# A rounded query copied behind the last scores instead of behind the matmuls, and relu's two instructions issued ahead of the chunk's output

## The chip, the cores and the metric

The kernel runs on one core of a Trainium2 chip. The metric is the device time of one execution in microseconds (us), lower is better; the time of a kernel is the median of several executions. Engines are named as in the profile: PE (matmul), PEld (its weight loads), DVE, ACT and POOL (elementwise work), SP (which issues the DMAs). Each engine works through its own queue in order.

## What is computed

Eight batches of eight heads of causal attention with a decay, over 576 tokens of 64 channels, and behind it a layer norm with a two-layer network of width 512 to 2048 and back, with a residual:

```python
scores = (q @ k.T) / 8 + cum[:, None] - cum[None, :]     # cum = cumsum(log(clip(f)))
attn = softmax(where(causal, -1e9, scores))
x = (attn @ v) laid out as (batch, 576, 512)
out = x + max(layernorm(x) * g @ w_ch1, 0) @ w_ch2
```

## The kernel before, in words

**Two kinds of work on one PE.** The kernel interleaves the attention of 64 heads with the network, which takes 18 chunks of 256 tokens (`NCHUNK`), each in 16 steps of 128 hidden channels (`FT`). Time is cut into slots: a head has four, t = 1 to 4, and slot t computes the scores of the row block t (slot 1 those of blocks 1 and 0; block 4 is 128 rows by 576 columns). Beside its attention each slot carries one step of the network, so that a chunk ends every 16 slots, which is every fourth head. After the last head the remaining steps run by themselves.

**What sets the order.** Nothing reorders the instructions: `ORDERS` (line 51) holds strings of letters, and the loop over the slots calls `piece(c)` for every letter of the string that holds at that slot. Letters issue instructions on several engines; on each engine they stand in the order of the string. The third string holds from slot 67 on, the fourth slot of head 16. Heads 0 to 15 (`NFULL`) do their matmuls in full float32. From head 16 on, the operands are split into a rounded part and a remainder; these heads are called late heads here.

**The letters that matter**, for a late head n in slot t:
- `Q`: `qk_mm`. Two matmuls for each block: `hi` against `hi` (L384, rounded q over the remainder of q, against rounded k twice) and `kl` against `xq` (L385, the remainder of k and two rows of the decay, against rounded q and two rows of ones). `xq` is one buffer for all heads.
- `S`, `e`, `B`: softmax. DVE adds the mask and takes the maximum (L425, twice for block 4, whose columns come in two halves), ACT the exponential (L436), DVE the reciprocal of the sum (L441, L442), POOL the product (L443).
- `T`, `d`, `V`: DVE transposes the last slot's block (L463, L465), SP writes it to HBM (L478) and reads it back transposed two slots on (L486).
- `H`, `l`, `o`: the transposed block is rounded by ACT (L501); its remainder comes from DVE (L506) and POOL (L515, two instructions).
- `F`, `a`: ACT copies half of a finished attention output (L649), DVE adds the other half (L660).
- `M`: the 12 matmuls of the first layer's step (L699 to L701), each taking 128 channels of `x`, rounded or remainder.
- `N`: `moe.second()`, the 6 matmuls of the second layer (L721 to L723) of the step before; at the chunk's end also `chunk_out`: two DVE instructions on `acc` (L798) and their DMAs.
- `A`: attention times values (L608), in slots 1 and 3.
- `P`: rounds the values on DVE (L362), in slot 2.
- `x`: `queries_copy`, in slot 4: ACT copies rounded q of the next head from `hi` to `xq` (L353), 64 x 576.
- `r`, `m`: relu of the first layer, rounded by ACT (L707), and its remainder by DVE (L712). Both read the PSUM tile of `M`; the next slot's `N` reads what they write.
- `b`: statistics of the rows; `R`: `moe.rest()`, with the split of the next chunk's `x` (L682 on ACT, L684 on DVE); at the chunk's end it splits the last two tiles, which the next slot's `M` needs.
- `k`: in slots 1 and 3 the next head's k or q is rounded (L339, L347 on ACT) and its remainder taken (L342, L356 on POOL), from a DMA into the single buffer `raw` (L325).

Of the kernel before, what the change touches and what calls it, by code (L numbers as in the profile page):

```python
# [50 lines left out]
ORDERS = [  # L51
    (0, "WwQsSthAeMrgFBmlLNPaXRf"),
    (37, "WwkQSTstAMhPeHlgNFrxfmBoDLRbaXdV"),
    (67, "kQSTeBHloFaMNAPxrmbRLdDVX"),
]


# [1022 lines left out]
```

## Time and profile before

| what | us |
|---|---|
| median of 3 runs (lowest to highest) | 1253.78 (1245.69 to 1289.03) |
| the profiled execution's own time | 1248.68 |
| its span, first to last instruction | 1246.9 |
| PE busy in the span | 1150.8 |
| DVE, ACT, POOL busy | 759.5, 641.0, 633.9 |
| late heads' slots, about | 214 to 1017 us of the span |

Rows of the timeline read: start, duration, engine, line, operation, output and inputs, shape; in brackets how long the engine was idle just before, and what released it. Matmuls overlap, so the end of one is modelled and lies behind the start of the next.

### The profile page before, as it was taken

Reading aid. Unit: us, or ns where it says so; the run is one execution under the profiler, and the core shown is the slowest. Engines: PE = TensorE matmul, PEld = TensorE weight load, DVE = VectorE, ACT = ScalarE, POOL = GpSimd, SP = SyncE. Lnnn points to the kernel's source line nnn. Section 1 sums busy time; section 2 is a strip of 40 time slices with the busy share of each in tenths; the row PEclk is TensorE's granted clock in tenths of the full one; section 3 lists DMA queues with packets and bytes.
Section 4 is the critical chain, followed back from the end, with each engine's and each line's share of the span. In section 5 each row is a group of like instructions: output and inputs, shape, how many; then the busy total and the mean of one; then the engine's idle time right before and its main releaser. Section 6 shows DMA issues by size and latency. Waiting matters only on the chain.

```text
span 1246.9 us, 24808 instructions
## 1 busy us (share of the span) xinstructions
PE 1150.8 (92%) x7648; PEld 1017.4 (82%) x7648; DVE 759.5 (61%) x2706; ACT 641.0 (51%) x1648; POOL 633.9 (51%) x966
## 2 busy tenths in 40 slices
PE   8889999999888999989899989898998999999998
PEld 6557888888787888888788878787887889999997
DVE  6777773666767766767667676766776762222222
ACT  5887575545555555655555555555555542112111
POOL 3545344566657666666666666666666551000000
PEclk9999999999999999999999999999999999999999
DMA  6555532657676776767675767677776751110100
GB/s 187 148 153 168 141 109 64 182 164 204 181 198 190 208 194 188 206 178 216 184 212 168 219 177 211 171 217 194 201 190 197 215 155 50 52 34 18 51 27 26
DMA packets 252724, 194.80 MB, mean 156 GB/s; under 512 B 83888, under 2 KB 231344, under 8 KB 252592
## 3 DMA queue, kind: packets, MB, share of 16 engines
q1 hardware_dynamic: 252592, 193.22, 55.7%
q8 instruction: 61, 1.00, 0.3%
q14 instruction: 71, 0.58, 0.2%
HBM read 126.79 MB, written 66.36 MB: 155 GB/s over the span
## 4 chain that ended last, share of the span: by engine, by line
PE 57%; ACT 14%; DVE 11%; DMA 7%; issue 7%; POOL 2%; SPq 1%; ACTq 0%; DVEq 0%; POOLq 0%
PE h L699 7%; PE h L700 7%; PE h L701 7%; PE acc L721 7%; PE acc L722 7%; PE acc L723 7%; PE o L608 5%; ACT ph L501 5%; ACT p L436 3%; DVE p L425 3%; PE s L385 2%; DMA pd<-pb 2%; ACT xq L353 2%; ACT ot L649 2%; PE s L384 2%
## 5 line engine op out<-in xcount | busy, mean ns | idle before, releaser
L436 ACT ACTIVATE p<-p,st 64x64 f32<-64x64 f32 (+4 forms) x320 | 179.2, 560 | 343.6 <-DVE st L425 284.9
L443 POOL TENSOR_SCALAR p<-p,st 64x64 f32<-64x64 f32 (+4 forms) x320 | 171.1, 539 | 360.6 <-DVE st L442 231.7
L700 PE MATMUL h<-x,w1h 128*128 128x256 f32 x1152 | 327.9, 285 | 5.0 <-DVE x L684 5.0
L699 PE MATMUL h<-x,w1h 128*128 128x256 f32 x1152 | 331.2, 287 | 0.6 <-DVE st L425 0.4
L701 PE MATMUL h<-x,w1l 128*128 128x256 f32 x1152 | 325.9, 283 | 0.0
L712 DVE SCALAR_TENSOR_TENSOR hh<-h,hh 128x256 fp32r<-128x256 f32 x288 | 121.4, 421 | 208.8 <-ACT hh L707 208.7
L721 PE MATMUL acc<-w2h,hh 128*128 128x512 f32 x576 | 230.6, 400 | 0.1
L722 PE MATMUL acc<-w2l,hh 128*128 128x512 f32 x576 | 229.8, 399 | 0.0
L700 PEld LDWEIGHTS h<-x,w1h 128*128 128x128 f32 x1152 | 219.9, 191 | 10.6 <-DVE x L684 7.5
L723 PE MATMUL acc<-w2h,hh 128*128 128x512 f32 x576 | 226.9, 394 | 0.0
L699 PEld LDWEIGHTS h<-x,w1h 128*128 128x128 f32 x1152 | 219.3, 190 | 6.6 <-issue 0.9
L701 PEld LDWEIGHTS h<-x,w1l 128*128 128x128 f32 x1152 | 220.4, 191 | 0.0
L707 ACT ACTIVATE hh<-h 128x256 fp32r<-128x256 f32 x288 | 109.0, 378 | 181.4 <-PE h L701 178.4
L425 DVE CUSTOM_DVE_ANT_0 p<-s,mask 64x64 f32<-64x64 f32 (+4 forms) x320 | 130.5, 422 | 100.7 <-PE s L385 93.6
L515 POOL TENSOR_TENSOR pt<-pt,ph 128x128 fp32r<-128x128 f32 x192 | 186.1, 987 | 6.9 <-ACT ph L501 6.9
L385 PE MATMUL s<-kl,xq 66*128 66x288 f32 (+4 forms) x288 | 82.8, 309 | 55.3 <-ACT xq L353 55.3
L723 PEld LDWEIGHTS acc<-w2h,hh 128*128 128x128 f32 x576 | 109.7, 190 | 25.5 <-DVE hh L712 0.2
L721 PEld LDWEIGHTS acc<-w2h,hh 128*128 128x128 f32 x576 | 110.6, 192 | 14.6 <-ACT hh L707 0.3
L722 PEld LDWEIGHTS acc<-w2l,hh 128*128 128x128 f32 x576 | 110.7, 192 | 12.1
L385 PEld LDWEIGHTS s<-kl,xq 66*128 66x128 f32 (+1 forms) x288 | 52.3, 181 | 71.1 <-ACT xq L353 68.7
L784 POOL TENSOR_SCALAR sv<-sv 128x2 f32<-128x2 f32 x18 | 3.9, 214 | 199.5 <-DVE sv L768 199.4
L501 ACT CAST ph<-pt 128x768 fp32r<-128x768 f32 x96 | 94.0, 979 | 5.0 <-DMA pt<-pd 4.5
(86 smaller groups left out, 1891.0 us busy)
## 6 DMA issues: line engine op xcount, KB each, us to landing
raw<-in_qk_dram SPq DMA_DIRECT2D x96, 288.0 KB
pt<-pd SPq DMA_DIRECT2D x192, 144.0 KB
pd<-pb SPq DMA_DIRECT2D x96, 192.0 KB
pt<-pd SPq DMA_DIRECT2D x192, 96.0 KB
wr<-in_w_dram SPq DMA_DIRECT2D x32, 512.0 KB
pd<-pb SPq DMA_DIRECT2D x48, 320.0 KB
pd<-pb SPq DMA_DIRECT2D x48, 256.0 KB
vr<-in_v_dram SPq DMA_DIRECT2D x64, 160.0 KB
```

Of the source, the lines that this page charges most:

```text
L385: mm(sp, xq, kl, start=False, stop=True)
L425: nc.vector.tensor_tensor_reduce(out=pt[:m, a:z], in0=sp, in1=mask[:m, max(0, off + a) : max(0, off + a) + z - a], scale=-SCALE, scalar=3. ...
L436: nc.scalar.activation(pt[:m, :w], pt[:m, :w], AF.Exp, bias=st[:m, i : i + 1], scale=-1.0, accum_out=st[:m, 2:3])
L443: nc.gpsimd.tensor_scalar(out=pt[:m, :w], in0=pt[:m, :w], scalar1=st[:m, 3:4], scalar2=1.0, op0=ALU.mult, op1=ALU.mult)
L501: nc.scalar.copy(out=h.ph[t], in_=h.pt[t].bitcast(F32))
L515: nc.gpsimd.tensor_tensor(out=pt[:, :, r, :], in0=pt[:, :, r, :].bitcast(F32), in1=ph[:, :, r, :].bitcast(F32), op=ALU.subtract)
L699: mm(ph, w1h[:, k, fs], c.x[k][:, 0, :], start=(k == 0), stop=False)
L700: mm(ph, w1h[:, k, fs], c.x[k][:, 1, :], start=False, stop=False)
L701: mm(ph, w1l[:, k, fs], c.x[k][:, 0, :], start=False, stop=(k == KT - 1))
L721: mm(c.acc[i], h[:, 0, ts_], w2h[:, j, :], start=(j == 0), stop=False)
L722: mm(c.acc[i], h[:, 0, ts_], w2l[:, j, :], start=False, stop=False)
L723: mm(c.acc[i], h[:, 1, ts_], w2h[:, j, :], start=False, stop=(j == FT - 1))
```

## The change

One string of `ORDERS` is changed, the one that holds from slot 67 to the end:

```diff
@@ -51,7 +51,7 @@
 ORDERS = [
     (0, "WwQsSthAeMrgFBmlLNPaXRf"),
     (37, "WwkQSTstAMhPeHlgNFrxfmBoDLRbaXdV"),
-    (67, "kQSTeBHloFaMNAPxrmbRLdDVX"),
+    (67, "kQxSTeBHloFaMPrmNAbRLdDVX"),
 ]
```

`x` moves from behind `P` to right behind `Q`. `P`, `r` and `m` move ahead of `N` and `A`. The rows of PE, POOL and SP stand in the same order as before; only ACT and DVE have rows that moved.

On ACT, the fourth slot of a late head, which is also the last step of a chunk; before (`p_4` is the block of scores, `ph` the rounded transposed block, `ot` the half output, `hh` the relu's output, `x_2` and `x_3` the next chunk's last tiles):

```order
L707 ACTIVATE hh_14_10016<-h_14_9991 128x256
L436 ACTIVATE p_4_10036,st_4_10037<-p_4_10036,st_4_10037 128x576
L501 CAST ph_45_10046<-pt_45_9971 128x1152
L649 COPY ot_0_10051<-o_2_10010 64x320
L353 CAST xq<-hi_9846 64x576
L707 ACTIVATE hh_15_10074<-h_15_10054 128x256
L682 CAST x_2_10077<-xr_2_9717 128x256
L682 CAST x_3_10080<-xr_3_9777 128x256
```

and the same place with the change:

```order
L707 ACTIVATE hh_14_10004<-h_14_9991 128x256
L353 CAST xq<-hi_9846 64x576
L436 ACTIVATE p_4_10037,st_4_10038<-p_4_10037,st_4_10038 128x576
L501 CAST ph_45_10047<-pt_45_9971 128x1152
L649 COPY ot_0_10052<-o_2_10013 64x320
L707 ACTIVATE hh_15_10068<-h_15_10055 128x256
L682 CAST x_2_10077<-xr_2_9717 128x256
L682 CAST x_3_10080<-xr_3_9777 128x256
```

The copy to `xq` (L353) has moved up three rows, ahead of the exponential; the relu and the splits stand one row nearer to the exponential. This happens in the fourth slot of 47 heads.

On DVE, the first slot of the next head, where the finished chunk is put out; before (`xt` is the chunk's output, `acc` its PSUM sums):

```order
L441 TENSOR_SCALAR st_0_9173<-st_0_9173 64x1
L442 RECIPROCAL st_0_9173<-st_0_9173 64x1
L798 SCALAR_TENSOR_TENSOR xt_0_8898<-acc_0_8324,rs_8901,xt_0_8898 128x512
L798 SCALAR_TENSOR_TENSOR xt_1_9024<-acc_1_8325,rs_8901,xt_1_9024 128x512
L712 SCALAR_TENSOR_TENSOR hh_0_9218<-h_0_9185,hh_0_9218 128x256
L425 ISA p_2_9227,st_2_9228<-s_2_0_9224,mask 128x320
```

and with the change:

```order
L441 TENSOR_SCALAR st_0_9173<-st_0_9173 64x1
L442 RECIPROCAL st_0_9173<-st_0_9173 64x1
L712 SCALAR_TENSOR_TENSOR hh_0_9198<-h_0_9185,hh_0_9198 128x256
L798 SCALAR_TENSOR_TENSOR xt_0_8898<-acc_0_8329,rs_8901,xt_0_8898 128x512
L798 SCALAR_TENSOR_TENSOR xt_1_9024<-acc_1_8330,rs_8901,xt_1_9024 128x512
L425 ISA p_2_9227,st_2_9228<-s_2_0_9224,mask 128x320
```

The relu's remainder (L712) has changed places with the two output instructions (L798). It does so at 12 chunk ends; `P`'s rounding of the values meets no other DVE row and stays where it stood.

## The prediction

> **What bounds the kernel now.** I read the page's first part, then the list of who waited for whom, then the timeline of one head engine by engine.
>
> ```profile
> span 1246.9 us, 24808 instructions
> PE 1150.8 (92%) x7648; PEld 1017.4 (82%) x7648; DVE 759.5 (61%) x2706; ACT 641.0 (51%) x1648; POOL 633.9 (51%) x966
> ```
>
> PE is busy for all but 1246.9 - 1150.8 = 96.1 us, and no other engine is above 61%. So a change pays only as far as it shortens PE's idle time. The list of waits says where that lies in the late heads:
>
> ```profile
> PE s L385 <- ACT xq L353: 55.3, 46, 2.1
> PE o L608 <- POOL vv L365: 15.2, 12, 1.3
> PE h L700 <- DVE x L684: 5.0, 12, 0.4
> ```
>
> (Total us, times, longest.) The largest wait is for the copy that the change moves. It comes 46 times, so in all but two of the late heads. The next two come 12 times each, once for each chunk's end. The timeline of an ordinary head shows how the wait arises:
>
> ```profile
> 750.99 0.30 PE L385 MATMUL s<-kl,xq 66*128 66x288 f32 x1
> 753.94 0.25 PE L384 MATMUL s<-hi 128*128 128x192 f32 x1
> 755.27 0.36 PE L385 MATMUL s<-kl,xq 66*128 66x192 f32 x1 [1.07 <-ACT xq L353]
> 757.07 0.40 PE L721 MATMUL acc<-w2h,hh 128*128 128x512 f32 x1
> 759.00 0.57 PE L608 MATMUL o<-pt,vv 128*64 128x256 f32 x4
> 752.29 0.78 ACT L436 ACTIVATE p<-p,st 128x576 f32<-128x576 f32 x1 [1.67 <-DVE st L425]
> 753.06 1.14 ACT L501 CAST ph<-pt 128x1152 fp32r<-128x1152 f32 x1
> 754.22 0.42 ACT L649 COPY ot<-o 64x320 f32<-64x320 f32 x1
> 754.55 0.67 ACT L353 CAST xq<-hi 64x576 fp32r<-64x576 f32 x1
> 755.24 0.38 ACT L707 ACTIVATE hh<-h 128x256 fp32r<-128x256 f32 x1
> ```
>
> The head's last scores (the old `xq`'s last reader) end at 750.99 + 0.30 = 751.29. From then on the copy could run, but it stands behind the exponential, the cast and the half output, and starts at 754.55. PE has the rest of that slot (2.6 us of `M` and `N`) and then needs `xq` from 753.94 on; it gets it at 755.27. Without a wait the two matmuls start 0.10 us apart, as in an early late head whose `xq` was ready:
>
> ```profile
> 214.37 0.26 PE L384 MATMUL s<-hi 128*128 128x192 f32 x1
> 214.47 0.27 PE L385 MATMUL s<-kl,xq 66*128 66x192 f32 x1
> ```
>
> So one wait costs 755.27 - 753.94 - 0.10 = 1.23 us, 0.16 more than the 1.07 listed as idle (the matmul in front counts as busy to its modelled end). All 46: 55.3 + 46 x 0.16 = 62.7 us.
>
> **The copy moved ahead.** It now starts when the last scores end, 751.29, and ends near 751.96. The exponential cannot start before 752.29, because DVE's second half of the mask ends only then: ACT was idle for 1.67 us there. The copy (0.67 us) fits into the 1.00 us between, so the exponential, the cast (which POOL and DVE wait for) and the half output stay where they were. PE asks for `xq` 2 us after the copy has ended. The cover is thus ACT's idle time; if it were gone, the exponential would slip by at most 0.67.
>
> **What is late next.** Take PE 1.23 us earlier from 755.27 on. Its next waits are for the relu, its remainder, and POOL's remainder of the transposed block:
>
> ```profile
> 754.76 0.48 DVE L660 TENSOR_TENSOR xs<-o,ot 64x320 f32<-64x320 f32 x1
> 755.66 0.42 DVE L712 SCALAR_TENSOR_TENSOR hh<-h,hh 128x256 fp32r<-128x256 f32 x1 [0.42 <-ACT hh L707]
> 754.42 2.42 POOL L515 TENSOR_TENSOR pt<-pt,ph 128x384 fp32r<-128x384 f32 x2
> ```
>
> The relu moves up by the copy's 0.69 us (755.24 to 754.55) and ends at 754.93; PE wants it at 757.07 - 1.23 = 755.84. Its remainder can then start when L660 ends, 755.24, and end at 755.66; PE wants it two matmuls later, at 756.3. POOL does not move: it ends at 756.84, and PE wants that at 759.00 - 1.23 = 757.77. All three keep 0.6 to 0.9 us. In slots 2 to 4 everything starts from PE's own scores and moves up with it, the POOL wait for the values (15.2 us) unchanged with it. The full 1.23 us (1.35 where 1.20 is listed) stays.
>
> **Except at the chunk's end.** There PE needs the split of the next chunk's `x` in the same slot:
>
> ```profile
> 739.88 0.28 PE L699 MATMUL h<-x,w1h 128*128 128x256 f32 x1
> 740.57 0.39 PE L700 MATMUL h<-x,w1h 128*128 128x256 f32 x1 [0.41 <-DVE x L684]
> 738.07 0.67 ACT L353 CAST xq<-hi 64x576 fp32r<-64x576 f32 x1
> 738.76 0.38 ACT L707 ACTIVATE hh<-h 128x256 fp32r<-128x256 f32 x1
> 738.16 0.48 DVE L660 TENSOR_TENSOR xs<-o,ot 64x320 f32<-64x320 f32 x1
> 739.18 0.42 DVE L712 SCALAR_TENSOR_TENSOR hh<-h,hh 128x256 fp32r<-128x256 f32 x1 [0.54 <-ACT hh L707]
> 739.52 0.99 DVE L684 TENSOR_TENSOR x<-xr,x 128x256 fp32r<-128x256 f32 x1
> 740.44 0.41 DVE L684 TENSOR_TENSOR x<-xr,x 128x256 fp32r<-128x256 f32 x1
> 738.95 1.28 POOL L515 TENSOR_TENSOR pt<-pt,ph 128x512 fp32r<-128x512 f32 x1
> ```
>
> The same subtraction takes DVE 0.99 us and then 0.41; the long one ends 0.28 us after POOL's (738.95 + 1.28 = 740.23), and PE goes on right behind it. So what PE waits for here is POOL, which the change does not move. PE would come 1.35 us earlier and wait for the same moment: gain nothing at 12 heads, 12 x 1.35 = 16.2 us. The bounds of this term are 0 and 16.2; I take 0, since L684 could start only about 0.6 us earlier (738.9), on top of POOL's start.
>
> The Trainium skill, "SBUF — State Buffer", section "SBUF: two separate sides", says that DVE (with two SBUF inputs) and GpSimd lock a shared port pair, and whichever starts first holds it for its whole instruction. The 0.99 against 0.41 agrees. By that rule these 12 heads gain nothing as long as POOL starts first, the sum's own 0.
>
> **Relu's remainder ahead of the output (12 times).** In the first slot after a chunk's end:
>
> ```profile
> 742.42 1.41 DVE L798 SCALAR_TENSOR_TENSOR xt<-acc,rs,xt 128x512 f32<-128x512 f32 x2
> 743.75 0.41 DVE L712 SCALAR_TENSOR_TENSOR hh<-h,hh 128x256 fp32r<-128x256 f32 x1
> 744.13 0.49 DVE L425 CUSTOM_DVE_ANT_0 p<-s,mask 128x320 f32<-128x320 f32 x1
> ```
>
> The three instructions fill 742.42 to 744.13 in either order, so the next scores' mask starts no earlier. PE's next `N` gets the remainder 1.3 us earlier, which it did not wait for; the two output DMAs start some 0.4 us later, which nobody reads. Bounds: 12 x 0.41 = 4.9 us either way; I take 0. `P`, and `r` on ACT against `N` and `A`, pass nothing on their queues: 0.
>
> **The sum.** 62.7 - 16.2 = 46.5 us off the profiled execution's 1248.68: 1202.2, and I say 1203 us. That execution lies 5.1 below the median of 1253.78; I predict its level, so 4% below the median.
>
> **The rivals.**
>
> (a) The splits get ahead of POOL. If DVE's L684 starts at 738.9, just before POOL's 738.95, both may run first, and PE gains at the 12 heads as well, up to 14 us: 1188. It is a race of 0.05 us, and both tiles must win it. Chance 0.13.
>
> By the Trainium skill's rule quoted above, from "SBUF — State Buffer", the first to start decides, so it allows this as well as its opposite.
>
> (b) The clock. After some chunk ends PE runs at half its clock:
>
> ```profile
> 606.30:610.00 3.70, 3.70 (x16) 3.12 (x15) 2.64 (x12) 1.15 (x5) 1.92 (x3) 0.54 0.04 14
> 603.90:609.90 6.00, 5.46 (x25) 0.72 0.31 91
> 738.70:744.70 6.00, 5.50 (x39) 1.00 0.40 129
> 400.00:466.40 66.40, 60.17 (x402) 54.36 (x401) 46.56 (x170) 37.41 (x91) 43.55 (x63) 1.00 0.72 198
> 466.40:534.40 68.00, 61.78 (x402) 55.64 (x401) 46.14 (x170) 37.56 (x91) 43.70 (x63) 0.97 0.70 193
> ```
>
> (Stretch, length, PE's busy time and more; the clock is the third number from the end, the DMA share the second.) Windows of 6 us behind the 12 chunk ends read 0.72 in four cases and 1.00 in eight; one of each is quoted. A chunk with such a stretch takes 68.0 us instead of 66.4. With the change PE's idle time at the chunk's end comes in one piece of some 0.41 + 1.35 = 1.8 us instead of two pieces. The sum assumes as many low stretches as before; were the other eight to fall too, it would be 8 x 1.6 = 13 us more: 1216. Chance 0.08.
>
> The Trainium skill, "TensorE: Matmul & The Clock Gate", "HAM oscillation", puts the drop at idle gaps beyond a window of some 3.4 us. By that rule no gap of 1.8 us would trip it; gaps of 1.19 and 0.42 do here, so the measurement decides.
>
> (c) Transfers set the pace. The DMA share differs by head, and two waits on transfers are near:
>
> ```profile
> 765.50:781.70 16.20, 15.00 (x101) 13.64 (x100) 11.25 (x41) 8.63 (x22) 10.48 (x13) 1.00 0.83 224
> ACT hi L347 <- DMA raw<-in_qk_dram: 24.6, 16, 3.2
> ACT ph L501 <- DMA pt<-pd: 4.5, 4, 2.3
> ```
>
> (Total us, times, longest, in the two lower rows.) Here the DMA share is 0.83. ACT already waits for `raw` in 16 heads and PE does not feel it. If the fullest heads, two of each four, could not shrink, 2 x 1.3 x 12 = 31 us of the gain would go: 1233. Against it: the block's reading is issued and used within the same PE time. Chance 0.13.
>
> (d) PE's stall only changes its name, with another late producer at the same place: about 1249. Each of the margins above would have to be wrong by over 0.6 us. Chance 0.04.
>
> (e) Slower: the copy holds up the exponential. POOL's remainder hangs on it and has 0.9 us to spare. PE loses beyond that, and the gain of 1.3 is eaten when the exponential slips by 2.2 us; at 3 us the time is 1248.7 + 46 x 0.8 = 1285. That needs a copy of 1.00 + 3 us against the measured 0.67. Chance 0.02.
>
> **How the numbers follow.** The forecast, 0.60, has 1192 to 1214 to itself (the 4.9 us, and a few low-clock stretches more or fewer). With (a) and (b) it makes 0.81 for faster by over 2%, that is below 1228.7; about 2% is what a measurement of this kernel can tell from no change. (c) and (d) make 0.17 within 2%, (e) 0.02. The range reaches from just below (a) to just short of (c)'s middle: 1186 to 1230.
>
> **What would show it.** Right: the wait of L385 for L353 is gone from PE's list, L353 starts at the end of the last L385, the exponential follows the second mask as before, and an ordinary head takes 1.2 to 1.35 us less. At chunk ends PE's wait for L684 grows from 0.4 to about 1.8 us. (a) shows as L684 at 0.41 us twice with POOL's L515 behind it; (b) as more stretches of clock 0.5; (c) as longer waits of L501 and L347 with PE idle behind them. The forecast is wrong if PE shows a new wait in ordinary heads, for L707, L712 or L515.

## The result, and the profile after

The changed kernel takes 1203.78 us (median of 4 runs, 1202.59 to 1208.0); the kernel before took 1250.88 beside it (4 runs). The ratio is 0.9643, with a 95% interval of 0.9593 to 0.9692: 3.6% faster. The prediction said 1203. A few executions ran in a slower state whatever the kernel (one of the kernel before at 1289.03 us, one of two_copies, an experiment, at 2790.09 us), and the ratios leave them out.

The page of the changed kernel, first part: the span and the busy time of the engines.

```profile
span 1202.3 us, 24761 instructions
PE 1147.1 (95%) x7648; PEld 1022.3 (85%) x7648; DVE 768.3 (64%) x2706; ACT 645.3 (54%) x1648; POOL 635.3 (53%) x966
```

PE works about as long as before (1150.8 us there) in a span that is 44.6 us shorter. What went is idle time. The list of waits of the changed kernel shows which (total us, times, longest):

```profile
PE o L608 <- POOL vv L365: 16.7, 12, 1.8
PE h L700 <- DVE x L684: 14.5, 12, 1.4
PE h L699 <- ACT x L682: 2.1, 10, 0.2
ACT p L436 <- DVE st L425: 176.4, 169, 3.9
ACT xq L353 <- PE s L385: 73.5, 46, 2.4
ACT hi L347 <- DMA raw<-in_qk_dram: 33.9, 29, 2.7
```

PE's wait of L385 for L353 (55.3 us before) is gone. ACT now waits for PE there instead (fifth row): the copy stands ready and starts when the last scores release its buffer. The split of the next chunk's `x` (L684), 5.0 us before, has grown to 14.5 in the same 12 places. ACT and PE in a head's fourth slot, PE at the start of the ordinary head behind it, and ACT's relu and PE's first use of it there:

```profile
783.99 0.67 ACT L353 CAST xq<-hi 64x576 fp32r<-64x576 f32 x1 [1.27 <-PE s L385]
784.90 0.78 ACT L436 ACTIVATE p<-p,st 128x576 f32<-128x576 f32 x1 [0.23 <-DVE st L425]
787.29 0.39 ACT L707 ACTIVATE hh<-h 128x256 fp32r<-128x256 f32 x1
783.60 0.30 PE L385 MATMUL s<-kl,xq 66*128 66x288 f32 x1
786.56 0.26 PE L384 MATMUL s<-hi 128*128 128x192 f32 x1
786.65 0.27 PE L385 MATMUL s<-kl,xq 66*128 66x192 f32 x1
788.37 0.40 PE L721 MATMUL acc<-w2h,hh 128*128 128x512 f32 x1
```

The last scores end at 783.60 + 0.30 = 783.90, the copy ends at 784.66, and PE wants it at 786.65, 2.0 us later. The two matmuls start 0.09 us apart. The exponential starts 1.00 us behind the last scores, as it did before, and ACT is still idle for 0.23 us ahead of it. From 786.56 to the next head's first scores at 801.07 PE is busy all the time by the profile (14.51 of 14.51 us), so no wait is left in this head.

A chunk's end, PE, DVE and POOL (the last row is the second of the two subtractions by itself):

```profile
707.50 0.38 PE L699 MATMUL h<-x,w1h 128*128 128x256 f32 x1 [0.21 <-ACT x L682]
709.26 0.39 PE L700 MATMUL h<-x,w1h 128*128 128x256 f32 x1 [1.38 <-DVE x L684]
707.38 0.42 DVE L712 SCALAR_TENSOR_TENSOR hh<-h,hh 128x256 fp32r<-128x256 f32 x1
707.72 1.83 DVE L684 TENSOR_TENSOR x<-xr,x 128x256 fp32r<-128x256 f32 x2
706.52 2.41 POOL L515 TENSOR_TENSOR pt<-pt,ph 128x384 fp32r<-128x384 f32 x2
707.66 1.27 POOL L515 TENSOR_TENSOR pt<-pt,ph 128x512 fp32r<-128x512 f32 x1
```

DVE's two splits take 1.83 us together, POOL's two subtractions end at 706.52 + 2.41 = 708.93, and PE goes on at 709.26. PE reached this place earlier and waits for the same moment.

The starts of each head's first scores give a period for each head. The first to the last of the 48 late heads took 789.4 us before (214.37 to 1003.78) and 744.5 after (214.16 to 958.63):

| head, within four | before, us | after, us |
|---|---|---|
| the three ordinary ones | 15.82, 16.29, 17.71 | 14.51, 14.85, 16.38 |
| with a chunk's end, full clock | 16.6 | 16.6 |
| with a chunk's end and a half-clock stretch | 18.2 | 18.2 (six of eight) |
| half-clock stretches, all late heads (behind the first four) | 5 (3) | 8 (8) |

A half-clock stretch is counted where matmuls of 128x256 start 0.23 us apart for some 3.5 us instead of 0.12. Two windows behind a chunk's end, one with a stretch and one without, and one around a stretch (window, length, PE's busy time and count, clock, DMA share, GB/s):

```profile
326.40:332.40 6.00, 4.61 (x18) 0.72 0.34 103
707.50:713.50 6.00, 4.62 (x31) 1.00 0.36 111
387.30:390.90 3.60, 3.60 (x15) 0.58 0.81 236
```

Six of the eight stretches follow a chunk's end. The other two, which start at 386.88 and 513.17, lie in the head ahead of one and follow a wait of PE for the values' remainder (L608, 1.65 and 1.67 us). In the trace's clock records each stretch lasts 3.41 us, and the eight starts are whole multiples of 3.413 us apart (455.15 - 328.85 = 126.30 = 37 x 3.413). So the stretches lie on a grid. In the late heads of the changed kernel PE is busy for 1.75 to 1.89 us in eight windows of this grid, and these are the eight ahead of the stretches; the next lowest window has 2.01 us. Two with a stretch behind them, then two at chunk ends without one:

```profile
383.46:386.88 3.42, 1.77 (x14) 1.00 0.36 87
451.73:455.15 3.42, 1.82 (x14) 1.00 0.79 219
707.74:711.15 3.41, 2.03 (x12) 1.00 0.43 127
834.04:837.46 3.42, 2.04 (x12) 1.00 0.49 143
```

At 707.74 a border of the grid cuts off the first piece of the chunk end's wait (0.21 us, up to 707.50); at 451.73 both pieces lie in one window. The grid is there in every profile with a stretch. In the late heads of the kernel before, the changed kernel and ten of the experiments all 56 stretches follow a window in which PE is busy for 57% or less. Seven windows of 51 to 56%, in five of the kernels, are followed by none, so this is not the whole rule.

### The profile page after: what moved, and what is told of

Read it like the earlier page. It is cut to its first block, busy times and chain, and to the rows that moved or that the text cites. A ratio compares the mean times of both kernels' runs of the same rounds, so it can differ in the third digit from the quotient of the medians.

```text
span 1202.3 us, 24761 instructions
## 1 busy us (share of the span) xinstructions
PE 1147.1 (95%) x7648; PEld 1022.3 (85%) x7648; DVE 768.3 (64%) x2706; ACT 645.3 (54%) x1648; POOL 635.3 (53%) x966
## 4 chain that ended last, share of the span: by engine, by line
PE 73%; DVE 8%; ACT 7%; POOL 4%; DMA 3%; issue 3%; SPq 1%; DVEq 0%; ACTq 0%; POOLq 0%
PE h L699 10%; PE h L700 10%; PE acc L721 9%; PE acc L722 9%; PE h L701 9%; PE acc L723 9%; PE o L608 5%; PE s L384 3%; PE s L385 2%; ACT p L436 2%; ACT ph L501 2%; PE s L382 2%; PE o L579 2%; POOL hi L356 1%; PE tr L524 1%
## 5 line engine op out<-in xcount | busy, mean ns | idle before, releaser
L700 PE MATMUL h<-x,w1h 128*128 128x256 f32 x1152 | 328.5, 285 | 14.5 <-DVE x L684 14.5
L699 PE MATMUL h<-x,w1h 128*128 128x256 f32 x1152 | 332.7, 289 | 2.7 <-ACT x L682 2.1
L712 DVE SCALAR_TENSOR_TENSOR hh<-h,hh 128x256 fp32r<-128x256 f32 x288 | 121.1, 420 | 186.5 <-ACT hh L707 185.8
L700 PEld LDWEIGHTS h<-x,w1h 128*128 128x128 f32 x1152 | 220.6, 191 | 20.1 <-DVE x L684 16.9
L699 PEld LDWEIGHTS h<-x,w1h 128*128 128x128 f32 x1152 | 219.8, 191 | 10.7 <-ACT x L682 4.1
L515 POOL TENSOR_TENSOR pt<-pt,ph 128x128 fp32r<-128x128 f32 x192 | 187.3, 995 | 8.3 <-ACT ph L501 8.3
L506 DVE TENSOR_TENSOR ph<-pt,ph 64x384 fp32r<-64x384 f32 x96 | 58.2, 607 | 57.6 <-ACT ph L501 50.9
L441 DVE TENSOR_SCALAR st<-st 128x1 f32<-128x1 f32 (+1 forms) x320 | 45.0, 141 | 73.3 <-ACT p L436 72.1
```

The lines of the kernel that those rows point to most:

```text
L515: nc.gpsimd.tensor_tensor(out=pt[:, :, r, :], in0=pt[:, :, r, :].bitcast(F32), in1=ph[:, :, r, :].bitcast(F32), op=ALU.subtract)
L699: mm(ph, w1h[:, k, fs], c.x[k][:, 0, :], start=(k == 0), stop=False)
L700: mm(ph, w1h[:, k, fs], c.x[k][:, 1, :], start=False, stop=False)
L712: nc.vector.scalar_tensor_tensor(out=h[:, 1, :], in0=ph, scalar=0.0, in1=h[:, 0, :].bitcast(F32), op0=ALU.max, op1=ALU.subtract)
```

## The experiments

Eleven kernels ran, in five groups; each ratio is against runs of the kernel before on the same chip. The first questions were which part of the change brings the gain, what holds PE at the chunk's end, what lowers the clock, and how much room the copy has.

### Which part: x_alone and relu_alone

```diff
# x_alone
-    (67, "kQSTeBHloFaMNAPxrmbRLdDVX"),
+    (67, "kQxSTeBHloFaMNAPrmbRLdDVX"),
# relu_alone
-    (67, "kQSTeBHloFaMNAPxrmbRLdDVX"),
+    (67, "kQSTeBHloFaMPxrmNAbRLdDVX"),
```

> Only the copy to xq moves (right behind the scores); P, r and m stand where they stood before. Theory (the whole gain is PE's wait for that copy): the time of the changed kernel, 1204 us within 4, and no wait of L385 for L353. Rival (the relu's order brings part of it): 1210 us or more, with the missing part in the 12 chunk ends, at most 12 x 0.41 = 5 us.

> Only P, r and m move ahead of N and A; the copy to xq stays behind the half output on ACT. Theory: the time of the kernel before, 1248 to 1251 us, with 46 waits of L385 for L353 and 55 us in them. Rival (the relu's remainder ahead of the output shortens the first slot after a chunk): 1243 us or less.

The copy alone takes 1202.44 us (1201.64 to 1204.09), ratio 0.9634 [0.9605, 0.9663], the same as the whole change (its profile has six half-clock stretches, with much the same waits at the chunk's end). The relu alone takes 1251.3 (1246.15 to 1261.23, 10 runs), ratio 1.0037 [1.0008, 1.0066]. PE's list in relu_alone is that of before:

```profile
PE s L385 <- ACT xq L353: 54.8, 46, 1.9
PE h L700 <- DVE x L684: 5.0, 12, 0.4
```

So the whole gain is the copy's, and the relu's move is worth nothing here. Whether it costs the 0.4% that the ratio shows is open: no wait has grown, and the profiled run has 7 half-clock stretches where before had 5, which would be about 3 us and may be chance.

### The chunk's end: split_first

At a chunk's end POOL's second subtraction (L515, 128x512) is left to DVE, which issues it behind the two splits. All lines below it move by 6: L690 is the split that was L684, L705 and L706 are L699 and L700.

```diff
+    held = []
...
+        last = t == 4 and moe.cur is not None and moe.cur.j == FT - 1
         for r in (slice(0, FIRSTS[t][0]), slice(FIRSTS[t][1], w)):
+            if last and r.start > 0:
+                held.append((pt, ph, r))
+                continue
             nc.gpsimd.tensor_tensor(
...
                 moe.rest()
+                while held:
+                    pt, ph, r = held.pop()
+                    nc.vector.tensor_tensor(
...
```

> The changed kernel, but at a chunk's end the second of POOL's two L515 subtractions is done by DVE instead, behind the two L684 splits. Theory (POOL's running subtraction keeps the split of x waiting): L684 takes 0.41 us twice, PE's wait at L700 falls from 1.4 us to 0.4 or less, 12 x 1.0 to 1.2 = 12 to 14 us, and with less idle time some of the 8 low-clock stretches go too: 1180 to 1193 us. Rival (the split is late by its own order on ACT and DVE): L684 stays where it is, the wait stays above 1 us and the time at 1204 us or above by DVE's extra 0.6 us per chunk.

It takes 1185.28 us (1183.84 to 1185.75), ratio 0.9493 [0.9465, 0.9521]. From split_first, PE's list, then a chunk's end on DVE and POOL:

```profile
PE h L706 <- DVE x L690: 3.3, 11, 0.3
```

```profile
697.57 0.75 DVE L690 TENSOR_TENSOR x<-xr,x 128x256 fp32r<-128x256 f32 x2
698.24 0.68 DVE L983 TENSOR_TENSOR pt<-pt,ph 128x512 fp32r<-128x512 f32 x1
696.38 1.17 POOL L521 TENSOR_TENSOR pt<-pt,ph 128x384 fp32r<-128x384 f32 x1
698.25 1.96 POOL L342 TENSOR_TENSOR kl<-raw,hi 64x576 fp32r<-64x576 f32 x1 [0.21 <-ACT hi L339]
```

The two splits take 0.75 us instead of 1.83, PE's wait falls from 14.5 us to 3.3, a chunk-end head from 16.6 or 18.2 us to 15.5, and the half-clock stretches from 8 to 1 (at 384.89, behind the wait for the values' remainder). So POOL's subtraction was what held the split. The Trainium skill, "SBUF — State Buffer", section "SBUF: two separate sides", has DVE (with two SBUF inputs) and GpSimd lock a shared port, so that one stands behind the other; 1.83 against 0.75 us agrees. Note the last row: POOL's L342 now stands behind DVE's and takes 1.96 us instead of the 1.43 that it takes on average in the changed kernel.

### The clock: fill_idle

Before the third tile of a chunk's first step PE gets 15 more matmuls of 128x256 into a half of a PSUM bank that nothing reads, some 2 us of work where it waited. Nothing is left out.

```diff
         for k in range(KT):
+            if k == 2 and j == 0 and c.n > 0 and "late" in pools and moe.fill_pe:
+                for i in range(15):
+                    mm(spare, w1h[:, 0, fs], c.x[0][:, 0, :], start=False, stop=False, skip_group_check=True)
             mm(ph, w1h[:, k, fs], c.x[k][:, 0, :], start=(k == 0), stop=False)
```

> The changed kernel with 15 extra matmuls (128x256, into the unused half of the same PSUM bank, never read) on PE at each chunk's first step among the late heads, where PE waits 1.4 to 1.6 us for the split of x. Each takes 0.12 us, 1.8 us in all. Theory (PE's idle time in one piece sets the low clock): the 8 stretches of about half clock fall to 2 or fewer and the time to 1204 - 6 x 1.6 = 1194 us. Rival (the low clock comes from something else, or from all the idle time of the head): as many stretches as before and 1204 to 1208 us, the extra work being up to 0.3 us longer than the wait.

It takes 1198.87 us (1195.63 to 1200.89), ratio 0.9602 [0.9569, 0.9634]. The first row is the added work in fill_idle, where PE otherwise stood idle:

```profile
643.45 1.96 PE L702 MATMUL h<-x,w1h 128*128 128x256 f32 x15
```

No half-clock stretch is left in its late heads (8 in the changed kernel), and the first to the last late head take 734.8 us instead of 744.5. The expectation was 1194 us. The 5 us by which the whole is faster than the changed kernel are fewer than the late heads' 9.7, since these began 6 us later in the profiled run (220.2 against 214.2). One of the 13 places that got the added work lies ahead of them, at 202.9 us; that is at most 2 us, and otherwise the same code there took 213.1 to 218.5 us in the other profiles, so the rest may be chance. So PE's idle time at the chunk's end is what lowers the clock behind it. Six chunk-end heads fell from 18.2 to 16.7 us, 9.1 of the 9.7 us, so such a stretch costs 1.5 us. The two stretches ahead of a chunk's end cost nothing: the pair of heads there takes 33.4 us with one (18.3 and 15.1) and 33.4 without (16.8 and 16.7), as PE then comes to the chunk's end later and waits less. Waits of the same length are followed by a stretch in some places and not in others, and in the changed kernel the grid above tells them apart.

### The copy's room: two_copies, three_copies, copy_behind_exp

```diff
# two_copies; three_copies has 3
+            for _ in range(2 if h.n > NFULL + 1 else 1):
                 nc.scalar.copy(out=h.xq[0:64, :], in_=h.hi[0:64, 0, :].bitcast(F32))
# copy_behind_exp, against the changed kernel
-    (67, "kQxSTeBHloFaMPrmNAbRLdDVX"),
+    (67, "kQSTexBHloFaMPrmNAbRLdDVX"),
```

> The changed kernel with the copy to xq done twice in a row (45 of the 47 times), so that ACT has about 1.25 us to do where 1.00 us are free between the last scores and the exponential. Theory: the exponential slips by about 0.25 us in each late head; the margins of PE behind it (0.54 to 0.7 us for the relu and its remainder, 0.8 us for POOL) cover that in ordinary heads; at the 12 chunk ends POOL's subtraction and with it the split of x comes 0.25 us later: 12 x 0.25 = 3 us, so 1205 to 1208 us. Rival (the exponential has no margin, each slip reaches PE): 46 x 0.25 = 11 us, 1215 us.

> The same with three copies in a row, about 1.85 us of ACT: the exponential slips by about 0.85 us, over the margin of the relu's remainder (0.54 us). Theory: PE waits some 0.3 us at L723 in 34 ordinary heads (10 us) and 0.85 us more at 12 chunk ends (10 us): about 1224 us, 1215 to 1232. Rival (the margins are wider than read): below 1212 us.

> The changed kernel with the copy right behind the exponential instead of ahead of it. Theory: the copy ends about 2.35 us behind the last scores and PE wants it at 2.65 us, so the wait of L385 stays away; but the cast, the half output, the relu and POOL's subtraction slip by 0.58 us, which just uses up the margins in ordinary heads and costs 0.58 us at each of the 12 chunk ends: about 1211 us, 1206 to 1216. Rival (only PE's wait for the copy counts): 1204 us as with the copy ahead.

Two copies take 1211.43 us (1207.96 to 1212.59, 3 runs), ratio 0.9685 [0.9633, 0.9736], above the 1205 to 1208 that was expected; there is no profile of it that could be read beside the others, so where the rest goes was not seen. Three copies take 1253.98 (1243.48 to 1261.33, 10 runs), ratio 1.0032 [0.9993, 1.0072]: the expectation of 1215 to 1232 was missed by over 20 us. The copy behind the exponential takes 1217.54 (1213.54 to 1220.17), ratio 0.9737 [0.9682, 0.9792], just above its 1206 to 1216.

From three_copies (its lines stand one lower: L354 the copy, L437 the exponential, L685 and L683 the splits), ACT in an ordinary head and PE's list:

```profile
760.69 2.08 ACT L354 CAST xq<-hi 64x576 fp32r<-64x576 f32 x3 [1.54 <-PE s L386]
762.68 0.77 ACT L437 ACTIVATE p<-p,st 128x576 f32<-128x576 f32 x1
```

```profile
PE h L701 <- DVE x L685: 16.5, 12, 1.4
PE h L700 <- ACT x L683: 14.3, 12, 1.3
PE acc L722 <- ACT hh L708: 10.0, 34, 1.1
```

The copies stand 0.7 us apart, so the exponential starts 2.08 us behind the last scores and slips by 2.08 - 1.00 = 1.08 us, not the 0.85 that was reckoned. Ordinary heads lose 0.58 to 0.74 us of it. In the changed kernel the relu has 0.69 us of room before PE wants it (788.37 - 787.29 - 0.39), and its remainder 0.53 to 0.66. The slip is longer than both, and PE's list now names the relu (L708) in 34 places: the loss is the slip beyond this room plus a little, as the theory had it for the remainder. What it had not reckoned with is the chunk's end, where ACT's rounding of the last tile of `x` (L683) is directly awaited by PE: two waits of 1.2 and 1.4 us in one slot, and 14 half-clock stretches instead of 8, seven of which last two windows of the grid (6.83 us). The late heads' stage rises by 49.5 us to 794.0. The 11 chunk-end heads in it give 27.7 of that: they hold 17 half-clock windows against 6, which at 1.5 us are some 17 us, and some 11 us are left for the waits, 1.0 a head. The other 36 heads give 21.8.

copy_behind_exp says the same in small. There the exponential stays where it was and the cast and the relu behind it slip by 0.56 to 0.58 us. Ordinary heads lose only 0.02 to 0.16 us. PE's list at the chunk's end shows where the rest goes:

```profile
PE h L700 <- DVE x L684: 15.1, 12, 1.3
PE h L699 <- ACT x L682: 7.8, 10, 0.8
```

The wait for ACT's rounding grows from 2.1 to 7.8 us, chunk-end heads lose 0.5 each and the stretches go from 8 to 10. So the place ahead of the exponential is worth some 14 us over the place right behind it (1217.5 against 1203.8).

### Beyond split_first: the other wait at the same rhythm

PE's largest wait is then the one for the values' remainder (L365 on POOL), once in four heads, behind six small operations on POOL (the rows' statistics, letter `L`, which start some 0.28 us apart). In split_and_late_rstd all these stand at the start of the slot instead of its end, on top of split_first, with the relu where it was before the change.

```diff
# split_and_late_rstd, on top of split_first
-    (67, "kQxSTeBHloFaMPrmNAbRLdDVX"),
+    (67, "kLQxSTeBHloFaMNAPrmbRdDVX"),
```

> Made to be faster: only the copy moved, as in x_alone; POOL's second subtraction at a chunk's end done by DVE, as in split_first; and POOL's small instructions for the layer norm's scale (letter L) moved from the slot's end to behind k in the next slot, so that the remainder of the values (L365), for which PE waits 12 times 1.3 us, no longer stands behind them. Theory: PE's 15 us of waits for L365 go: 1168 to 1174 us. Rival (the small instructions now hold up the product of the next block, L443, and through it PE): 1183 us or more, with another POOL wait on PE's list.

It takes 1186.88 us (1182.8 to 1191.81), ratio 0.9496 [0.9448, 0.9544]: no better than split_first, and not the 1168 to 1174 that was expected. The third heads fell from 16.38 to 14.85 us as expected, but chunk-end heads rose from 15.5 to 17.1. Its chunk's end:

```profile
697.74 0.39 PE L706 MATMUL h<-x,w1h 128*128 128x256 f32 x1 [0.68 <-DVE x L690]
699.31 0.39 PE L706 MATMUL h<-x,w1h 128*128 128x256 f32 x1 [0.94 <-DVE x L690]
695.50 0.88 DVE L506 TENSOR_TENSOR ph<-pt,ph 64x256 fp32r<-64x256 f32 x1 [0.70 <-ACT ph L501]
697.27 1.98 DVE L690 TENSOR_TENSOR x<-xr,x 128x256 fp32r<-128x256 f32 x2
697.57 1.40 POOL L342 TENSOR_TENSOR kl<-raw,hi 64x576 fp32r<-64x576 f32 x1 [0.33 <-ACT hi L339]
```

Here POOL's remainder of the next head's k (L342) starts between DVE's two splits, and the second one ends only behind it. In split_first the second split was first, by 0.3 us. The splits are late because DVE runs without a gap from L506 on, and L506 took 0.88 us instead of 0.50. POOL's product ran beside it; that this is the reason was not tested. Three more kernels followed this.

```diff
# late_remainder on top of split_and_late_rstd,
# split_first_late_remainder on top of split_first
             elif c == "m" and want:
-                moe.first_low()
+                if held:
+                    held.append(moe.step)
+                else:
+                    moe.first_low()
...
                 moe.rest()
+                if len(held) == 2:
+                    mm1_low(held.pop())
# split_first_rstd_later, on top of split_first
+                if slot is not None and n > NFULL and t == 3:
+                    run_later(RSTD)
...
-            elif c == "L":
+            elif c == "L" and not (slot is not None and n > NFULL and t == 2):
                 run_later(RSTD)
```

> The kernel of split_and_late_rstd (1186.88), in which at the chunk's end alone the relu's remainder on DVE is issued behind the two splits instead of ahead of them; nothing is left out. What it asks: what held the second split there. Theory: POOL's subtraction for the next head's k (1.40 us, two SBUF inputs) started 0.3 us behind DVE's first split and ahead of its second one (697.27 and 697.57), and DVE's second split stood behind it for 1.57 us; 0.42 us of remainder taken from ahead of them lets both splits start before it. Then PE's wait for the split falls from 17.9 us in 22 waits to under 6, the chunk-end heads go from 17.1 us to about 15.4, one or two of the three half-clock stretches go as well: 1186.9 - 11 x 1.3 - 2 = 1171, between 1166 and 1176. Rival 1: the splits are late because the earlier head's product on POOL is (everything shifted together); then the wait stays above 14 us and the time within 1183 to 1190. Rival 2: the remainder of the relu is late for the second layer instead; then PE shows a new wait for it of 0.3 us or more at 11 places, and the time is 1174 to 1180.

> The kernel of split_first (1185.28) with the same edit: at the chunk's end the relu's remainder on DVE behind the splits; nothing is left out. PE still waits there for the split in 11 places, 0.3 us each, and the splits start 0.42 us earlier at most (ACT's rounding of the last tile ends near the old start). Theory: 11 x 0.3 = 3.3 us less, 1182, between 1179 and 1185. Rival: nothing, since ACT's rounding of the last tile sets the second split, 1184 to 1187.

> The kernel of split_first (1185.28); in the third slot of a late head the small operations for the rows' statistics on POOL (six of some 0.28 us) are issued behind the values' remainder (L365) instead of ahead of it, and nowhere else; nothing is left out. split_and_late_rstd moved them in every slot and changed the first slot's order with them. Theory: what it lost at the chunk's end (17.1 us against 15.5) came from those other moves, which are not made here. Then the third heads fall from 16.38 to 14.85 us and the chunk-end heads stay at 15.5: 12 x 1.53 = 18 us less, 1167, between 1163 and 1172. Rival 1: the later operations themselves push POOL's work at the chunk's end, since DVE's second split waits there again; then PE's wait for the split is above 10 us and the time 1180 to 1188. Rival 2: PE without these two waits runs into transfers (L501 and L486 wait for them already); then half of the gain is left, 1174 to 1179.

| kernel | us (lowest to highest) | ratio [95%] | PE's wait for the split, us | DVE's piece of POOL's work, mean ns | chunk-end head, us |
|---|---|---|---|---|---|
| split_first | 1185.28 (1183.84 to 1185.75) | 0.9493 [0.9465, 0.9521] | 3.3 | 678 | 15.5 |
| split_and_late_rstd | 1186.88 (1182.8 to 1191.81) | 0.9496 [0.9448, 0.9544] | 17.9 | 782 | 17.1 |
| late_remainder | 1186.6 (1182.47 to 1189.4) | 0.9503 [0.9455, 0.955] | 9.0 | 1355 | 16.8 |
| split_first_late_remainder | 1199.98 (1198.76 to 1203.38) | 0.9622 [0.9585, 0.9659] | 1.9 | 1702 | 16.6 |
| split_first_rstd_later | 1181.97 (1179.0 to 1184.27) | 0.9474 [0.9413, 0.9535] | 8.8 | 1404 | 16.0 to 17.1 |

The theories of late_remainder and split_first_late_remainder fell. Each is to be compared with the kernel that it changes, split_and_late_rstd and split_first. The wait for the split did go down in both (fourth column), and the time did not. The groups by line show where it went, in split_first and then in split_first_late_remainder:

```profile
L983 DVE TENSOR_TENSOR pt<-pt,ph 128x512 fp32r<-128x512 f32 x12 | 8.1, 678 | 0.0
```

```profile
L985 DVE TENSOR_TENSOR pt<-pt,ph 128x512 fp32r<-128x512 f32 x12 | 20.4, 1702 | 0.0
```

The piece that DVE took over from POOL is the same instruction, and takes 1.70 us instead of 0.68. One of the twelve, in split_first_late_remainder:

```profile
897.01 0.41 DVE L718 SCALAR_TENSOR_TENSOR hh<-h,hh 128x256 fp32r<-128x256 f32 x1
897.35 1.79 DVE L985 TENSOR_TENSOR pt<-pt,ph 128x512 fp32r<-128x512 f32 x1
899.07 0.34 DVE L425 CUSTOM_DVE_ANT_0 p<-s,mask 128x192 f32<-128x192 f32 x1
897.17 1.43 POOL L342 TENSOR_TENSOR kl<-raw,hi 64x576 fp32r<-64x576 f32 x1
```

With the relu's remainder (L718) moved in between, POOL's L342 starts 0.18 us ahead of DVE's piece, which then stands behind it. The mask of the next head's scores, queued behind the piece on DVE, starts a good 1 us late, and the relu and its remainder behind that. In split_first the piece began 0.01 us ahead of L342 and POOL waited instead, for which PE's list shows no wait. PE's list in split_first_late_remainder names what it then waits for:

```profile
PE acc L727 <- ACT hh L713: 7.2, 9, 1.5
PE acc L729 <- DVE hh L718: 5.8, 11, 0.5
```

These rows are 13.0 us; split_first had 2.6 for the relu. The rest of the 14.7 us between the two kernels was not followed further.

split_first_rstd_later came out at the time of its first rival, and not at the 1163 to 1172 that was expected: third heads at 14.84 us as forecast, chunk-end heads up by 0.5 to 1.6, and PE's wait for the split at 8.8 us (the rival had said above 10). Its median is the lowest of the study, 1182 us, 21.8 us below the changed kernel, but its range overlaps that of split_first, so the two are not told apart.

## Why the prediction was right

**The wait and its 0.16 us more.** Right. Ordinary heads fell by 1.31, 1.44 and 1.33 us. The sum had 62.7 - 16.2 = 46.5 us for 34 waits, 1.37 each. x_alone shows that all of it is the copy's.

**The copy fits ahead of the exponential.** Right. The exponential starts 1.00 us behind the last scores before and after, and 0.23 us of ACT's idle time is left. With two more copies ahead of it, the ordinary heads lose what goes beyond the room of the relu and its remainder; the least of this room is 0.53 us, where the prediction had put the least of its margins at 0.6.

**Nothing at the chunk's end.** Right, and for the reason given. Full-clock heads stay at 16.6 us. The forecast of 1.8 us for the grown wait was near: 0.21 + 1.38 = 1.59 us in the chunk's end shown. split_first shows the cause by taking it away. Rival (a) was lost by a hair: POOL's second subtraction starts at 707.66 and DVE's split at 707.72, and the order is the same, by 0.04 to 0.06 us, at all 12 chunk ends. The prediction had called it a race of 0.05 us; that it came out this way was luck, since nothing in its rows could decide it.

**The relu's order: 0.** Right within the measurement; relu_alone leaves the 0.4% open.

**The clock, rival (b).** It came in part. Behind the first four late heads there are 8 stretches instead of 3. Six of the 8 follow a chunk's end and cost about 1.6 us each. At the other two the pair of heads takes 0.4 us more than elsewhere (18.3 and 15.1 us against 16.4 and 16.6), which fill_idle shows to be the longer wait for the values' remainder and not the clock. Together that gave back 10.4 - 3 x 1.6 = 5.6 us, inside the forecast's own range. fill_idle shows that PE's idle time at the chunk's end is the cause. The prediction's reason, one piece instead of two, fits the grid, though no run tests it: the idle time there is 1.6 us before and after (1.19 + 0.42, and 0.21 + 1.38), but it now lies within 2.0 us (707.29 to 709.26) instead of 3.0 (737.60 to 740.57) and so falls into one window of 3.41 us more often. The Trainium skill, "TensorE: Matmul & The Clock Gate", section "HAM oscillation", puts the drop at idle gaps beyond a window of some 3.4 us; here gaps of 1.4 to 1.7 us were enough, and with work in the chunk end's gap there was no drop, so the measurement decides.

**The transfers, rival (c).** They did not set the pace. ACT's wait for `raw` rose from 24.6 to 33.9 us, yet the heads with the fullest transfers shrank like the others (16.29 to 14.85). Rivals (d) and (e) did not come. Of (e), three_copies shows that the point from which it decides was put too far out: the whole gain is eaten when the exponential slips by 1.08 us, not by 2.2, because the chunk's end pays for it as well, in waits and in half-clock stretches.

**The sum.** 46.5 us predicted off the profiled span; 44.6 measured, of which the late heads have 44.9. There, 32 regular ordinary heads at 1.36 us are 43.5; the first four late heads went from 68.5 to 64.3; three ordinary heads that were longer before (16.83, 16.20 and 16.58 us) give 2.2 beyond the 1.36; the clock and those two pairs take 5.6 back. That makes 44.3, and one more ordinary head, which gained only 0.6, makes it 44.9. So the mechanism is the predicted one, but that the forecast came within 1 us is partly luck: beyond the sum's own rate the first four late heads gave some 2.8 us (two half-clock stretches fewer) and the three longer ones 2.2, which made up for most of the 5.6.

## What to carry to other kernels

Copy into a single buffer as soon as its last reader is done, if the engine that copies is idle there; price the move by its gap in the timeline, and then ask of each place, by rhythm, what that place would wait for next: the gain was full in three heads of four and nothing in the fourth. Where two engines work on SBUF side by side, an order that wins by a few hundredths of a microsecond is worth as much as a removed wait, and any edit ahead of it can turn it over: after each edit, compare the mean duration of the same instruction, not only the list of waits.

## What the runs showed of the hardware

- Which of DVE and POOL starts first decides who pays. DVE's subtraction of 128x512 took 0.68 us when it started 0.01 us ahead of POOL's L342 and 1.79 us when it started 0.18 us behind it; the Trainium skill's rule on the shared port ("SBUF — State Buffer", section "SBUF: two separate sides") agrees.
- The same subtraction of 128x512 took POOL 1.28 us (before the change, at the chunk's end) and DVE 0.68 (mean of 12 in split_first).
- Half-clock stretches of 3.41 us followed PE's idle time of 0.21 + 1.38 us at 6 of the 12 chunk ends in the changed kernel, and waits of 1.65 and 1.67 us in two other places. None followed a chunk's end when PE had work there (fill_idle).
- Within a profile the stretches start whole multiples of 3.413 us apart. In the changed kernel they follow the eight windows of this grid in which PE is busy least, 1.75 to 1.89 us; at 2.01 us and more none followed.
